# Turned heads scored on 32x32 tiles in 14 units, in an attention and MLP block on one core

## The chip, the cores and the metric

The kernel runs on one core of one Trainium2 chip. The metric is the device time of one execution in microseconds (us). Before the change it is 1140.88 us, the median of three runs (1139.4 to 1143.8). Engines are named as the profile names them: PE (TensorE matmuls), PEld (its weight loads), DVE (VectorE), ACT (ScalarE), POOL (GpSimd) and SP (SyncE, which issues most DMAs here).

## The reference

A token block of 2048 rows and 448 columns goes through an attention and an MLP in parallel, and both are added to the input:

```python
B, S, D, H = 1, 2048, 448, 16      # Dh = 28, F = 1792
xn = layernorm(x)
# attention: 16 query heads, one key head and one value head
q = (xn @ wq).reshape(B, S, H, Dh).transpose(0, 2, 1, 3)
k, v = xn @ wk, xn @ wv
p = softmax(einsum("bhqd,bkd->bhqk", q, k) * Dh ** -0.5)
a = einsum("bhqk,bkd->bhqd", p, v) merged over heads @ wo
# MLP on a second layernorm of xn
h = gelu(layernorm(xn) @ w1 + b1)
return x + a + h @ w2 + b2
```

All data are float32.

## The kernel before

**Stages.** The first stage (to about 66 us) normalises the input, projects queries, keys and values and writes the queries to DRAM (`qd`). The second stage (to 454 us) is the MLP. The third is attention. Matmuls with the large operands run as float32r, with each operand held as a rounded high part and a low part (`w1h` and `w1l`, `hh` and `hl`, the rows of `ks` and of the query tiles), so that three products stand for one. The order on every engine is the program's own (`manual_schedule`): each engine takes its instructions in the order in which the code issues them, and waits at one whose input or buffer isn't free.

**Units and steps.** Attention has 16 units: four chunks of 512 queries (`NCH`) times four groups of four heads (`NG`). A unit goes through the 16 key tiles of 128 in 8 steps of two key tiles, so there are 128 steps, n = 0 to 127. For a key tile and a head, a score matmul writes 128 keys by 512 queries into one PSUM bank (the line `pe.matmul(s, ...)`, L798), ACT takes the exp out of it into a tile `p` (L805), and `pv` (L708) multiplies `p` with the values. One step issues 8 float32 matmuls of `pv` in one burst, on four column tiles of 32; they belong to the step before. A string, `ORDER`, gives the order within a step letter by letter: s a score with its exp, m a maximum, t a turned score, P the burst, e a turned exp, n a piece of the unit's normalisation, o a piece of the output projection.

**Maxima.** The softmax's maximum of each query is found ahead by a second set of score matmuls with queries on the partitions (`max_stream`, L478) and a reduction of each on DVE (L479). They are issued in the MLP stage, `MLP_MAX` = 15 for each 46 steps of the MLP's own matmul stream, and the rest in attention, spread by `weight`. `load_max` transposes a unit's maxima (L461) and DMAs them, negated, into a row of the query tile that meets a row of ones in `ks`. So the score comes out with the maximum taken off.

**Turned heads.** In 7 of the 16 units (`TURNED`) the fourth head goes another way. Its scores are computed with the queries on the partitions (`turned_scores`, L730, four matmuls for each of four query tiles), DVE copies them out of PSUM and takes their maximum in the same instruction (L731), and ACT takes the exp in place (L750). Sixteen DMAs per query tile then regroup the rows (`regroup`, L746), so that DVE's 32x32 block transposes (`turn_blocks`, L757) make the tiles `p` that `pv` needs. Such a head needs neither maximum matmuls nor score matmuls.

**PSUM.** Of eight banks `mp` has three (named m: maxima, turned scores, output tiles, transposes), `sp` four (scores) and `op` one (the sum of `pv`).

**MLP.** `mlp1` makes a 128x512 piece of the hidden layer by 11 matmuls, GELU and rounding on ACT, and the low half `hl` on DVE (L524, put off to the next slot through `lows`). `mlp2` uses it two slots later. A slot is one such piece. There are 56.

**Ones.** Two rows of `ks` are set to one by GpSimd (`ones_rows`, L389) after the keys have been loaded.

Of the kernel before, what the change touches and what calls it, by code (L numbers as in the profile page):

```python
# [15 lines left out]
P = 128  # L16
# [10 lines left out]
MLP_MAX = 15  # L27
ORDER = "smsmstnsPemssmosmnsm"
TURNED = (3, 5, 7, 9, 11, 13, 15)
QB = 8  # L30
RAWS = 3
# [6 lines left out]
def block_kernel(ctx, tc, x, wq, wk, wv, wo, w1, b1, w2, b2, out):  # L38
# [82 lines left out]
    for t in qmt:  # L121
        pool.memset(f(t), 0.0)
    b1r = wqp.tile([NF, P], F32, name="b1r", bufs=1)
# [21 lines left out]
    def split_weights():  # L145
        for i in range(2):
            split_small(kvraw[:, :, i, :], lambda w, i=i: w[:, :, 32 * i + 1:32 * i + 1 + DH])
# [159 lines left out]
    def w2_split(s):  # L307
        raw = wl_q.pop(0)
        ab = slice(2 * s, 2 * s + 2)
        act.activation(w2h[:, ab, :], raw, AF.Copy)  # L310
        dve.tensor_sub(w2l[:, ab, :], raw, f(w2h[:, ab, :]))

    def q_slot(c, i):
# [7 lines left out]
        def evac():  # L321
            qe = wqp.tile([P, 2, CW], F32R, name="qe", bufs=CT)
            at = slice(64 if i == 0 else 0, P)
            act.activation(qe[at, 0, :], ps[at, :], AF.Copy)
            vt = None
            if i == 0:
                vt = wqp.tile([32, CW], F32, name="vt", bufs=1)
                kl = wqp.tile([64, CW], F32R, name="kl", bufs=1)
                act.activation(ks[32:64, cols], ps[32:64, :], AF.Copy)
                act.activation(vt, ps[0:32, :], AF.Copy)  # L330
            dve.tensor_sub(qe[at, 1, :], ps[at, :], f(qe[at, 0, :]))
            if i == 0:
                dve.tensor_sub(kl[32:64, :], ps[32:64, :], f(ks[32:64, cols]))
                for dst, src in ((0, kl[32:64, :]), (64, kl[32:64, :]), (96, ks[32:64, cols])):
                    nc.sync.dma_start(f(ks[dst:dst + 32, cols]), f(src))
# [51 lines left out]
    def ones_rows():  # L387
        for r in (32, 96):
            pool.memset(f(ks[r:r + 1, :]), 1.0)  # L389

    later(3, 2, ones_rows, True)
# [4 lines left out]
    def load_m(u, j, qm=None, t=None):  # L396
        c, g = units[u]
        at = slice(0, CW) if t is None else slice(t * P, (t + 1) * P)
        cols = slice(c * CW + at.start, c * CW + at.stop)
        if qm is None:  # L400
            qm = qmt[heads.index((u, j)) % 3]
        for blk, i in ((1, 0), (2, 0), (0, 1), (3, 1)):
            nc.sync.dma_start(f(qm[32 * blk + 1:32 * blk + 1 + DH, at]), qd[i][DH * (4 * g + j):DH * (4 * g + j + 1), cols])
# [36 lines left out]
    def load_q(u):  # L440
# [6 lines left out]
        for blk, i in ((1, 0), (2, 0), (0, 1), (3, 1)):  # L447
            nh = heads_of(u)
            src = qd[i][4 * DH * g:4 * DH * g + DH * nh, cols].rearrange("(j r) n -> r j n", r=DH)
            nc.sync.dma_start(f(qs[32 * blk + 1:32 * blk + 1 + DH, 0:nh, :]), src)  # L450
# [6 lines left out]
    def load_max(u):  # L457
# [4 lines left out]
        mn = keep.tile([4 * CT, 2, P], F32R, name="mn", bufs=2)[0:nh * CT]  # L462
        act.activation(mn[:, 0, :], pm, AF.Copy, scale=-1.0)
        dve.scalar_tensor_tensor(mn[:, 1, :], pm, -1.0, f(mn[:, 0, :]), op0=ALU.mult, op1=ALU.subtract)
        nc.sync.dma_start(f(qs[32:33, 0:nh, :]), f(mn[:, 0, :]))
        nc.sync.dma_start(f(qs[96:97, 0:nh, :]), f(mn[:, 1, :]))

    def max_stream():
        for h, (u, j) in enumerate(heads):
# [5 lines left out]
            for t in range(CT):  # L475
                for n in range(4):
# [3 lines left out]
                    if (j, t, n) == (heads_of(u) - 1, CT - 1, 3):  # L480
                        mrs[u] = keep.tile([P, 4 * CT], F32, name="mr", bufs=10)
# [31 lines left out]
    def mlp1(c, ft):  # L513
# [10 lines left out]
        lows.append(lambda: dve.tensor_sub(hl, hr, f(hh)))  # L524

    def mlp2(c, ft, between):
# [4 lines left out]
        for k in range(CT):  # L531
# [11 lines left out]
            if k == 2 and lows:  # L543
                lows.pop(0)()
            yield

    def slot(n):
# [13 lines left out]
        else:  # L561
            if nxt:
                nxt()
            lows.pop(0)()

    lows, norms, maxed = [], {}, 0
# [34 lines left out]
    q3 = att.tile([P, CW], F32R, name="q3", bufs=1)  # L601
    pool.memset(f(q3), 0.0)
# [32 lines left out]
    def norm_jobs(u, po):  # L635
# [12 lines left out]
        else:  # L648
            nc.sync.dma_start(rc, oc[0:P:32, :])
            yield  # L650
            yield
# [68 lines left out]
    turned, tside = {}, Stream()  # L720

    def turned_scores(u):
        turned[u] = hbs = []
        nxt = TURNED.index(u) + 1
        for t in range(CT):
            raw = att.tile([P, 4, NT, 32], F32, name="raw", bufs=RAWS)
            m3 = att.tile([P, 8], F32, name="m3")
            for n in range(4):
                sc = mtile([P, CW])
                pe.matmul(sc, q3[:, t * P:(t + 1) * P], ks[:, n * CW:(n + 1) * CW], start=True, stop=True)  # L730
                dve.tensor_scalar(raw[:, :, 4 * n:4 * n + 4, :].rearrange("p r b i -> p b r i"),  # L731
                                  sc.rearrange("p (b r i) -> p b r i", r=4, i=32), SCALE, -3e38,
                                  op0=ALU.mult, op1=ALU.max, accum_out=m3[:, n:n + 1])
                if n == 3:
                    dve.tensor_reduce(m3[:, 4:5], m3[:, 0:4], axis=AX.X, op=ALU.max, negate=True)  # L735
                    tside.add(turned_exps(hbs, t, raw, m3))
                    if nxt < len(TURNED):
                        load_m(TURNED[nxt], 3, q3, t)
                yield

    def turned_exps(hbs, t, raw, m3):
        def regroup(r):
            if t % 2 == 0 and r == 0:
                hbs.append(half_tile())
            for a in range(4):
                nc.sync.dma_start(hbs[-1][32 * r:32 * r + 32, 4 * (t % 2) + a, :],  # L746
                                  raw[32 * a:32 * a + 32, r].rearrange("p b i -> p (b i)"))

        for r in range(4):
            act.activation(raw[:, r], raw[:, r], AF.Exp, bias=m3[:, 4:5], scale=1.0)  # L750
            regroup(r)
            yield
# [10 lines left out]
    load_m(TURNED[0], 3, q3)  # L763
    tq = Stream()
    for u in TURNED:
        tq.add(turned_scores(u))

    def o_wait(c, gs, tiles):
        for _ in range(8):
# [7 lines left out]
    weight = [0 if n >= len(steps) - LEAD else 8 if u in TURNED  # L777
              else 18 if u + 2 < NU else 12 for n, (u, kt) in enumerate(steps)]
    for n, (u, kt) in enumerate(steps):
        if n == 12:  # L780
            prep_wo()
        if u + 1 < NU:
            if kt == 0:
                load_q(u + 1)
        qs = qss[u]
        j = 0
        for what in ORDER:
            if what == "s":
                kk = kt + j // 4
                if u in TURNED and j % 4 == 3:  # L790
                    if j == 3:
                        p = pair_of()
                        turn_blocks(p, u, kt)
                        ps[u, kt, 3], ps[u, kt + 1, 3] = p[:, 0], p[:, 1]
# [16 lines left out]
            elif what == "t":  # L811
                if n >= 3:
                    tq.step()
            elif what == "e":
                if kt == (6 if u + 2 < NU else 10) and u + 1 < NU:
                    load_max(u + 1)
                tside.step()
            elif what == "n":
                side.step()
            elif what == "o":  # L820
# [7 lines left out]
            elif n > 0 and 2 * n % BURST == 0:  # L828
                for _ in range(BURST):
                    pv(*pvq.pop(0))  # L830
# [29 lines left out]
```

## Time and profile before

| what | us |
|---|---|
| median of three runs | 1140.88 |
| the profiled execution, its time | 1142.51 |
| the profiled execution, its span | 1140.7 |
| first score matmul of attention | 454.54 |
| first value burst | 460.24 |

The trace is of one execution. A row of the groups gives line, engine, operation, what it writes and reads, shapes and count, then busy time in us and the mean duration in ns, then the idle time of that engine just before and what ended it. Durations overlap, since a matmul's or an activation's tail runs beside the next one's start. So what an instruction costs a busy engine is read from start to start. The granted TensorE clock is 0.998 over the span.

### The profile page before, as it was taken

How to read it: one execution, taken by the hardware profiler on the slowest of the kernel's cores; microseconds unless marked ns; L12 is line 12 of the kernel's file. 1: busy time of each engine (PE TensorE's matmuls, PEld its weight loads, DVE VectorE, ACT ScalarE, POOL GpSimd, SP SyncE). 2: the span in 40 equal slices, each digit the busy share in tenths (PEclk: the TensorE clock that was granted, in tenths of full speed). 3: DMA queues.
4: the chain of work that ended last, by engine and by line, in shares of the span. 5: the costliest groups of instructions: out<-in, count | busy, mean ns of one | idle time of the engine just before them, and what ended most of it. 6: DMA issues, size and time to landing. Idle time of an engine off the chain costs nothing.

```text
span 1140.7 us, 17019 instructions
## 1 busy us (share of the span) xinstructions
PE 1122.8 (98%) x5905; PEld 729.7 (64%) x5905; DVE 867.1 (76%) x1600; ACT 689.6 (60%) x1290; POOL 109.3 (10%) x113
## 2 busy tenths in 40 slices
PE   9989999999999999999999999999999999999998
PEld 8768888888888888555554555544455554564454
DVE  7779889888888888777777777777667677777434
ACT  6753322221222222788888877888777888878974
POOL 5340000000002000002101101101101101101100
PEclk9999999999999999999999999999999999999999
DMA  9751100000000020332343342342433443442300
GB/s 287 200 181 51 43 15 17 17 17 18 17 17 17 17 49 18 86 82 75 97 100 78 101 111 76 105 100 74 103 97 84 102 101 76 106 104 65 85 24 33
DMA packets 65426, 86.82 MB, mean 76 GB/s; under 512 B 20566, under 2 KB 31980, under 8 KB 65212
## 3 DMA queue, kind: packets, MB, share of 16 engines
q1 hardware_dynamic: 63932, 85.16, 28.1%
q8 instruction: 47, 0.77, 0.3%
q10 hardware_dynamic: 1408, 0.57, 0.2%
q14 instruction: 39, 0.32, 0.1%
HBM read 44.05 MB, written 11.12 MB: 48 GB/s over the span
## 4 chain that ended last, share of the span: by engine, by line
PE 88%; DVE 4%; DMA 3%; ACT 2%; issue 1%; SPq 1%; POOL 0%; DVEq 0%; ACTq 0%; POOLq 0%
PE po L708 19%; PE m L478 18%; PE s L798 17%; PE ph L158 10%; PE m L535 4%; PE m L537 4%; PE m L533 4%; PE m L730 3%; DMA xh<-qd 2%; PE qp L158 2%; PE m L622 1%; PE m L624 1%; PE m L623 1%; PE ph L161 1%; DMA rc<-oc 1%
## 5 line engine op out<-in xcount | busy, mean ns | idle before, releaser
L479 DVE TENSOR_REDUCE mx<-m 128x1 f32<-128x512 f32 x912 | 593.2, 685 | 160.5 <-PE m L478 146.2
L805 ACT ACTIVATE p<-s 128x512 f32<-128x512 f32 x879 | 447.4, 614 | 94.3 <-PE s L798 94.2
L478 PE MATMUL m<-ks,qm 128*128 128x512 f32 x912 | 371.0, 407 | 3.5 <-POOL ks L389 2.4
L798 PE MATMUL s<-xh,ks 128*128 128x512 f32 x879 | 318.2, 407 | 2.8 <-ACT p L805 2.5
L708 PE MATMUL po<-p,vs 128*32 128x512 f32 x2048 | 247.9, 601 | 0.0
L478 PEld LDWEIGHTS m<-ks,qm 128*128 128x128 f32 x912 | 171.3, 188 | 108.5 <-issue 26.0
L798 PEld LDWEIGHTS s<-xh,ks 128*128 128x128 f32 x879 | 163.3, 188 | 86.6 <-ACT p L805 35.0
L519 ACT ACTIVATE hr<-ph,b1t 128x512 f32<-128x512 f32 x56 | 38.6, 689 | 277.3 <-PE ph L163 191.5
L708 PEld LDWEIGHTS po<-p,vs 128*32 128x32 f32 x2048 | 53.9, 109 | 120.2 <-issue 114.1
L750 ACT ACTIVATE raw<-raw,m 128x512 f32<-128x512 f32 x112 | 82.7, 738 | 9.9 <-DVE m L735 9.0
L533 PE MATMUL m<-w2h,hh 128*128 128x448 f32 x224 | 82.4, 368 | 0.0
L535 PE MATMUL m<-w2l,hh 128*128 128x448 f32 x224 | 81.6, 364 | 0.0
L537 PE MATMUL m<-w2h,hl 128*128 128x448 f32 x224 | 81.5, 364 | 0.0
L731 DVE TENSOR_SCALAR_CACHE_REDUCE raw<-m 128x512 f32<-128x512 f32 x112 | 76.2, 680 | 0.0
L660 POOL TENSOR_TENSOR oc<-oc,tr 128x512 f32<-128x512 f32 x15 | 19.4, 1294 | 589.0 <-DMA tr<-ld 206.6
L757 DVE STREAM_TRANSPOSE p<-half 128x512 f32<-128x512 f32 x112 | 72.6, 687 | 1.6 <-PE po L708 1.6
L158 PE MATMUL ph<-xh,w1h 128*128 128x512 f32 x168 | 66.5, 396 | 0.0
L158 PE MATMUL ph<-xh,w1l 128*128 128x512 f32 x168 | 66.4, 395 | 0.0
L158 PE MATMUL ph<-xl,w1h 128*128 128x512 f32 x168 | 66.0, 393 | 0.0
L626 DVE TENSOR_TENSOR acc<-acc,m 128x448 f32<-128x448 f32 x22 | 13.6, 621 | 51.5 <-PE m L624 51.5
L730 PE MATMUL m<-ks,q 128*128 128x512 f32 x112 | 47.2, 422 | 3.4 <-DVE mx L479 3.4
L535 PEld LDWEIGHTS m<-w2l,hh 128*128 128x128 f32 x224 | 42.0, 188 | 6.3
(141 smaller groups left out, 964.4 us busy)
## 6 DMA issues: line engine op xcount, KB each, us to landing
half<-raw SPq DMA_DIRECT2D x448, 64.0 KB
qm<-qd SPq DMA_DIRECT2D x228, 56.0 KB
xh<-qd SPq DMA_DIRECT2D x36, 224.0 KB
qd<-qe SPq DMA_DIRECT2D x24, 256.0 KB
xh<-qd SPq DMA_DIRECT2D x28, 168.0 KB
tr<-ld SPq DMA_DIRECT2D x56, 64.0 KB
raw<-in_B_w_dram SPq DMA_DIRECT2D x7, 448.0 KB
out_dram<-acc SPq DMA_DIRECT2D x14, 224.0 KB
```

The lines of the kernel that those rows point to most:

```text
L158: pe.matmul(ps, w, v, start=(n == 0), stop=False)
L478: pe.matmul(pm, qm[:, t * P:(t + 1) * P], ks[:, n * CW:(n + 1) * CW], start=True, stop=True)
L479: dve.tensor_reduce(mx[:, CT * j + t, n:n + 1], pm, axis=AX.X, op=ALU.max)
L533: pe.matmul(m2[k], hh[:, ts], w2h[:, ft, :], start=(ft == 0), stop=False)
L535: pe.matmul(m2[k], hh[:, ts], w2l[:, ft, :], start=False, stop=False)
L537: pe.matmul(m2[k], hl[:, ts], w2h[:, ft, :], start=False, stop=(ft == NF - 1))
L708: pe.matmul(po[32 * j:32 * j + 32, :], vs[:, kt, :], ps.pop((u, kt, j)), start=(kt == 0), stop=(kt == NT - 1))
L730: pe.matmul(sc, q3[:, t * P:(t + 1) * P], ks[:, n * CW:(n + 1) * CW], start=True, stop=True)
L731: dve.tensor_scalar(raw[:, :, 4 * n:4 * n + 4, :].rearrange("p r b i -> p b r i"), sc.rearrange("p (b r i) -> p b r i", r=4, i=32), SCALE, ...
L750: act.activation(raw[:, r], raw[:, r], AF.Exp, bias=m3[:, 4:5], scale=1.0)
L798: pe.matmul(s, ks[:, kk * P:(kk + 1) * P], qs[:, j % 4, :], start=True, stop=True)
L805: act.activation(p, s, AF.Exp, scale=SCALE)
```

## The change

The set of turned units grows from 7 to 14 (units 2 to 15). Their scores are computed in float32 by 16 matmuls on 32x32 tiles for one query tile of 128: row group a of the array holds 32 queries of block a, column group r takes every fourth key block of 32, and the results land in four banks in the layout that the block transposes need. So the 16 regrouping DMAs go. Float32 keys come from `kf`, the sum of the high and low rows of `ks`, made once by GpSimd; queries come from `q3s`, summed from DMAs of both parts (`load_q3`, 8 DMAs a unit). A query's maximum is now spread over four partitions, so two small transposes on PE with a reduction and two copies on DVE join it (`turned_max`, letters c and d). The rounds (letter R) stand in odd steps from n = 7 to 117, the maxima in even steps from unit 2 on, and a turned exp (letter x) is issued twice a step. All scores, maxima, rounds and transposes take their banks in turn from one ring of seven. `MLP_MAX` goes to 20; the MLP's low halves `hl`, and the low halves `w2l` but the first, are computed by GpSimd. `ks` is set to one as a whole at the start, with 28 rows of keys copied instead of 32.

```diff
-MLP_MAX = 15
-ORDER = "smsmstnsPemssmosmnsm"
-TURNED = (3, 5, 7, 9, 11, 13, 15)
+MLP_MAX = 20
+ORDERS = ("scsmsmsxPdemsxmsmnsmson", "ssmssxRPesxmsnsson")
+TURNED = tuple(range(2, 16))
...
+    pool.memset(f(ks), 1.0)
...
-        dve.tensor_sub(w2l[:, ab, :], raw, f(w2h[:, ab, :]))
+        (pool if s else dve).tensor_sub(w2l[:, ab, :], raw, f(w2h[:, ab, :]))
...
-    def ones_rows():
-        for r in (32, 96):
-            pool.memset(f(ks[r:r + 1, :]), 1.0)
-
-    later(3, 2, ones_rows, True)
...
-        lows.append(lambda: dve.tensor_sub(hl, hr, f(hh)))
+        pool.tensor_sub(hl, hr, f(hh))
...
-        return att.tile([P, QB, CW], F32, name="half", bufs=3)
+        return att.tile([P, QB, CW], F32, name="half", bufs=4)
+
+    banked = 0
+
+    def mtile(shape):
+        nonlocal banked
+        banked += 1
+        return mp.tile(shape, F32, name="m") if banked % 7 in (1, 2, 3) else sp.tile(shape, F32, name="s")
...
+    for n in range(4):
+        cols = slice(n * CW, (n + 1) * CW)
+        pool.tensor_add(kf[:, cols], f(ks[:, cols]), kt_[:, n, :])
+    kq = kf.rearrange("p (b r i) -> p b r i", r=4, i=32)
...
+    def load_q3(u):
+        c, g = units[u]
+        for i, q in enumerate(q3p):
+            src = qd[i][DH * (4 * g + 3):DH * (4 * g + 4), c * CW:(c + 1) * CW].rearrange("r (t g j) -> g r t j", g=4, j=32)
+            for b in range(4):
+                nc.sync.dma_start(q[32 * b:32 * b + DH, :, :], src[b])
+        q3s[u] = att.tile([P, CT, 32], F32, name="q3s", bufs=2)
+        pool.tensor_add(q3s[u], q3p[0], q3p[1])
+
+    def turned_round(u, t):
+        if t % 2 == 0:
+            turned.setdefault(u, []).append(half_tile())
+        half = turned[u][-1]
+        banks = [mtile([P, CW]) for _ in range(4)]
+        for r in range(4):
+            for a in range(4):
+                pe.matmul(banks[a][32 * r:32 * r + 32, :], q3s[u][32 * a:32 * a + DH, t, :],
+                          kq[32 * a:32 * a + DH, :, r, :], start=True, stop=True)
+        m3 = att.tile([P, 4], F32, name="m3")
+        for a in range(4):
+            dve.tensor_scalar(half[:, 4 * (t % 2) + a, :], banks[a], SCALE, -3e38,
+                              op0=ALU.mult, op1=ALU.max, accum_out=m3[:, a:a + 1])
+        maxes.append(turned_max(half, t, m3))
+
+    def turned_max(half, t, m3):
+        pt = mtile([4, P])
+        pe.transpose(pt, m3, ident)
+        mq = att.tile([4, 4, 32], F32, name="mq", bufs=1)
+        dve.tensor_reduce(mq[:, 0, :], pt.rearrange("a (r j) -> a j r", r=4), axis=AX.X, op=ALU.max, negate=True)
+        dve.tensor_copy(mq[:, 1:4, :], mq[:, 0:1, :].to_broadcast([4, 3, 32]))
+        yield
+        pb = mtile([P, 4])
+        pe.transpose(pb, mq.rearrange("a r j -> a (r j)"), ident[0:4, 0:4])
+        mb = att.tile([P, 4], F32, name="mb")
+        dve.tensor_copy(mb, pb)
+        for a in range(4):
+            exps.append((half[:, 4 * (t % 2) + a, :], mb[:, a:a + 1]))
+        yield
+
+    def turned_exp():
+        if exps:
+            raw, m = exps.pop(0)
+            act.activation(raw, raw, AF.Exp, bias=m, scale=1.0)
...
-    weight = [0 if n >= len(steps) - LEAD else 8 if u in TURNED
-              else 18 if u + 2 < NU else 12 for n, (u, kt) in enumerate(steps)]
+    weight = [0 if n >= len(steps) - LEAD else 2 if u == 0 or u == 1 and n % 2 == 0 else 1 if u == 1 or n % 2 == 0
+              else 0 for n, (u, kt) in enumerate(steps)]
+    rounds = {8 * (u - 2) + 7 + 2 * t: (u, t) for u in TURNED for t in range(CT)}
...
-        for what in ORDER:
+        if u in TURNED:
+            while exps and kt == 0:
+                turned_exp()
+            p = pair_of()
+            turn_blocks(p, u, kt)
+            ps[u, kt, 3], ps[u, kt + 1, 3] = p[:, 0], p[:, 1]
+        for what in ORDERS[n % 2 if n > 6 else 0]:
...
-                s = mtile([P, CW]) if (n == 0 and j < 3) or (maxed == total and j % 2) else sp.tile([P, CW], F32, name="s")
+                s = mtile([P, CW])
...
+            elif what == "R":
+                if n in rounds:
+                    turned_round(*rounds[n])
+            elif what in "cd":
+                if maxes:
+                    next(maxes[0])
+                    if what == "d":
+                        maxes.pop(0)
+            elif what == "x":
+                turned_exp()
+                if kt == 14 and len(exps) == 1:
+                    turned_exp()
...
+            elif what == "P":
+                for _ in range(BURST if n else 0):
+                    pv(*pvq.pop(0))
```

Counted over the kernel: 912 maximum and 912 score matmuls become 800 and 800, 112 turned score matmuls become 56 rounds of 16, 448 regrouping DMAs go, and the turned exps, the copies out of PSUM and the block transposes on DVE go from 112 to 224 each.

More of the change, by code (lines that the diff above doesn't have):

```diff
@@ L542, in mlp2 @@
                 between()
-            if k == 2 and lows:
-                lows.pop(0)()
             yield
@@ L718, in pv @@
                 oside.add(o_wait(c, range(NG), range(CT if c < NCH - 2 else 2)))
[L720 to L744, printed above, removed]
-            for a in range(4):
[L746 to L752, printed above, removed]
+    turned, q3s, maxes, exps = {}, {}, [], []
```

70 lines of the change are left out of this document (29 added, 41 removed).

## The prediction

> **What bounds the kernel now.** I read the page first (shares of the span, then the chain that ended last), then the busy times by stage, then the groups by line, and last the timeline of two steps of the attention stage.
>
> ```profile
> span 1140.7 us, 17019 instructions
> PE 1122.8 (98%) x5905; PEld 729.7 (64%) x5905; DVE 867.1 (76%) x1600; ACT 689.6 (60%) x1290; POOL 109.3 (10%) x113
> ...
> PE 88%; DVE 4%; DMA 3%; ACT 2%; issue 1%; SPq 1%; POOL 0%; DVEq 0%; ACTq 0%; POOLq 0%
> ```
>
> TensorE is busy all the time and is 88% of the chain. A share over the whole span hides the stages, so here they are (columns: stretch, length, then busy us and count on PE, PEld, DVE, ACT, POOL; granted clock; DMA).
>
> ```profile
> 66.00:454.30 388.30, 385.13 (x1761) 323.80 (x1760) 337.17 (x534) 97.28 (x148) 26.83 (x21) 1.00 0.10 29
> 460.20:504.50 44.30, 44.29 (x246) 23.38 (x245) 32.46 (x61) 34.91 (x71) 0.00 (x0) 1.00 0.32 77
> 504.50:550.20 45.70, 44.94 (x246) 23.33 (x245) 33.41 (x65) 39.56 (x80) 7.61 (x7) 1.00 0.38 95
> 550.20:1077.60 527.40, 521.94 (x2929) 269.86 (x2928) 386.04 (x755) 425.18 (x828) 41.65 (x39) 1.00 0.37 93
> 1077.60:1128.30 50.70, 50.70 (x306) 27.95 (x305) 16.59 (x28) 37.96 (x76) 2.59 (x2) 1.00 0.06 18
> 1128.30:1140.70 12.40, 7.68 (x47) 4.60 (x46) 6.06 (x14) 2.11 (x5) 0.00 (x0) 0.98 0.21 75
> ```
>
> The first stretch is the MLP; the others are attention, cut at the value bursts that open steps 0, 8, 16, 116 and 127 (a step is two key tiles of one unit; a unit has 8). In the MLP DVE stands at 337 of 388 us and ACT is nearly free. In attention ACT is at 80%, DVE at 73%. A step of a turned unit, on PE:
>
> ```profile
> 694.51 0.63 PE L798 MATMUL s<-xh,ks 128*128 128x512 f32 x2
> ...
> 695.90 0.40 PE L730 MATMUL m<-ks,q 128*128 128x512 f32 x1
> 696.22 1.92 PE L708 MATMUL po<-p,vs 128*32 128x512 f32 x16
> 698.08 1.20 PE L798 MATMUL s<-xh,ks 128*128 128x512 f32 x4
> 699.11 0.40 PE L478 MATMUL m<-ks,qm 128*128 128x512 f32 x1
> 699.35 0.47 PE L798 MATMUL s<-xh,ks 128*128 128x512 f32 x1
> ...
> 700.47 1.06 PE L708 MATMUL po<-p,vs 128*32 128x512 f32 x8
> ```
>
> From burst to burst are 4.25 us. A burst lasts 1.86 (696.22 to 698.08), it starts 0.32 after the last matmul's start, and a 512-column matmul costs about 0.235: nine of them with a burst are 4.1, so PE sets the pace. ACT at the same place:
>
> ```profile
> 691.73 0.71 ACT L750 ACTIVATE raw<-raw,m 128x512 f32<-128x512 f32 x1
> 692.35 1.05 ACT L805 ACTIVATE p<-s 128x512 f32<-128x512 f32 x2
> 694.94 2.07 ACT L805 ACTIVATE p<-s 128x512 f32<-128x512 f32 x4 [1.55 <-PE s L798]
> 696.87 0.74 ACT L750 ACTIVATE raw<-raw,m 128x512 f32<-128x512 f32 x1
> ```
>
> A score matmul started at 694.51 and its exp at 694.94: 0.43 of latency. Exps follow each other by 0.48 (696.87 less 694.94, over 4), a turned exp takes 0.62 of the queue (692.35 less 691.73), and before the row of four ACT idled 1.55 us.
>
> **The change part by part.** *Front.* The 2048-column memset of ks moves ahead of GpSimd's first split:
>
> ```profile
> 1.73 1.46 POOL L122 MEMSET qm<- 128x512 f32 x3
> 6.25 0.29 POOL L141 TENSOR_SCALAR wah<-kvraw 128x112 fp32r<-128x112 f32 x1 [3.06 <-DMA kvraw<-in_A_wv_dram]
> ...
> 66.24 3.65 POOL L389 MEMSET ks<- 1x2048 f32 x2 [3.24 <-DVE qe L331]
> ...
> 69.95 0.50 PE L478 MATMUL m<-ks,qm 128*128 128x512 f32 x1 [2.44 <-POOL ks L389]
> ```
>
> One such memset is 3.65/2 = 1.8 us and fits the 3.06 idle (nothing; at most 1.8 if the weights landed earlier). The two late ones go, and with them PE's wait of 2.4 (0 if another wait stands right behind): -2.4.
>
> *MLP.* Of 1288 steps of the MLP stream, 20 instead of 15 in 46 carry a maximum matmul: 140 more, at 0.235, +33. First burst: 460.2 + 33 - 2.4 = 491. Cover on DVE:
>
> ```profile
> L479 DVE TENSOR_REDUCE mx<-m 128x1 f32<-128x512 f32 x912 | 593.2, 685 | 160.5 <-PE m L478 146.2
> L524 DVE TENSOR_TENSOR hl<-hr,hh 128x512 fp32r<-128x512 f32 x56 | 40.4, 722 | 0.0
> L311 DVE TENSOR_TENSOR w2l<-raw,w2h 128x896 fp32r<-128x896 f32 x7 | 7.6, 1080 | 0.0
> L667 POOL TENSOR_TENSOR otl<-oc,oth 128x512 fp32r<-128x512 f32 x15 | 19.3, 1288 | 4.4 <-ACT oth L664 3.2
> ```
>
> A reduction costs DVE 593.2/912 = 0.65, so 140 add 91, and 47 leave for GpSimd: 381 of 419 us, still below PE. GpSimd takes 1.29 for a low half (row L667), 56 of them are 72 us in 419, and the matmul that reads one comes two slots (14 us) later: nothing. Without that cover DVE would pace the stage at about +10.
>
> *Attention, units 0 and 1.* Unit 0: 8 scores, 6 maxima and a burst, 14 x 0.235 + 1.95 = 5.24 a step, 43 with its ends (44.3 now). Unit 1 gets four rounds as well; a pair of its steps has 16 exps and 4 turned exps, 16 x 0.48 + 4 x 0.62 = 10.2 of ACT. At the densest ACT in the trace,
>
> ```profile
> 1050.00:1100.00 50.00, 49.71 (x284) 25.26 (x283) 20.91 (x39) 43.23 (x85) 3.99 (x4) 1.00 0.28 72
> ```
>
> 43.23 of 50 or 86%, that is 11.8, and the queue below makes it 12.5: 49 for the unit (45.7 now).
>
> *The round.* 16 float32 matmuls take the place of four 0.235 ones for seven turned heads, and of 32 (16 maxima, 16 scores) for seven new ones. The nearest row is the burst, also float32 and also on tiles:
>
> ```profile
> 642.26 0.13 PEld L708 LDWEIGHTS po<-p,vs 128*32 128x32 f32 x4 [0.30 <-issue]
> 642.69 0.13 PEld L708 LDWEIGHTS po<-p,vs 128*32 128x32 f32 x4 [0.30 <-issue]
> 643.66 0.28 PE L461 MATMUL m<-ident,mr 128*12 128x128 f32 x1
> 643.69 0.48 PE L478 MATMUL m<-ks,qm 128*128 128x512 f32 x1
> ```
>
> Each of 8 float32 matmuls is recorded twice (x16), and four column tiles go together in waves 0.43 apart. If all 16 tiles run together, a round is two waves: a burst less two waves, 1.86 - 0.86 = 1.0 until the next burst starts. If the four row groups go one after another it is 8 waves, 1.86 + 4 x 0.43 = 3.6. I take 1.0, because the four column tiles share their waves without loss. The switch into tiles is the 0.32 against 0.235, about 0.1 a round. The Trainium skill, TensorE: Matmul & The Clock Gate, section Measured speedup vs the span model, gives 10.6 times for 16 such tiles; against 16 x 0.86 in series that is an estimate of 1.3 a round, and 1198 in all by it; no run here shows it. The two small transposes a round adds cost PE 0.03 to 0.06 (643.66 to 643.69).
>
> *A pair of steps from unit 2 on* (all units turned): 12 scores, 3 maxima, 2 bursts, 1 round, 2 transposes. PE: 15 x 0.235 + 2 x 1.95 + 1.1 + 0.1 = 8.6. ACT: 12 x 0.48 + 4 x 0.62 = 8.24. DVE, by these rows,
>
> ```profile
> L731 DVE TENSOR_SCALAR_CACHE_REDUCE raw<-m 128x512 f32<-128x512 f32 x112 | 76.2, 680 | 0.0
> L731 DVE DVE_READ_ACCUMULATOR raw<-m 128x1 f32 x112 | 9.2, 82 | 0.0
> L757 DVE STREAM_TRANSPOSE p<-half 128x512 f32<-128x512 f32 x112 | 72.6, 687 | 1.6 <-PE po L708 1.6
> L735 DVE TENSOR_REDUCE m<-m 128x1 f32<-128x4 f32 x28 | 4.4, 158 | 1.0
> L805 ACT ACTIVATE p<-s 128x512 f32<-128x512 f32 x879 | 447.4, 614 | 94.3 <-PE s L798 94.2
> ```
>
> 3 x 0.65 + 4 x 0.76 + 4 x 0.65 (72.6/112) + about 0.6 for a reduction and two copies a round (an estimate from row L735's 0.16) = 8.2. Three engines stand within 0.4 us of each other, so the order decides. A pair takes 21 banks of the ring of seven, and a bank's next user waits for its reader. Counting seven back along the two orders, the round's fourth bank is that of the even step's last score: the round waits for that exp, which stands behind one turned exp in ACT's queue. The even step's second maximum (just ahead of its burst) waits for the exp of the odd step's second score behind the burst. That closes a loop, from the round's fourth matmul:
>
> - round 1.0, burst 1.86, latency 0.43, exp 0.48, turned exp 0.62, exp done 0.61 (row L805), PE wakes 0.06: 5.06
> - the maximum, switch and burst 0.32 + 1.86, transpose and a maximum 0.27, latency 0.43, exp 0.48, turned exp 0.62, exp 0.48, exp done 0.61, wake 0.06: 5.13
>
> The wake is read where a matmul waited for its bank:
>
> ```profile
> 1005.58 0.19 PEld L478 LDWEIGHTS m<-ks,qm 128*128 128x128 f32 x1 [0.20 <-DVE mx L479]
> 1005.64 0.44 PE L478 MATMUL m<-ks,qm 128*128 128x512 f32 x1
> ```
>
> Together 10.2 a pair, 1.6 over PE's sum. ACT then works 8.24 of 10.2, 81%, which the trace has reached; 8.6 would ask 96%, which no stretch shows. What ends last in this stage turns from PE to exps that start late after each burst.
>
> *Sum.* First burst 491, unit 0 43, unit 1 49, fifty pairs 510; 10 output tiles (12 matmuls of 448 columns, 0.235 x 448/512 = 0.2 each; of their 2.4 about 1.7 not in PE's waits) 17, and the copy that 13 units add on ACT, 0.6 like an exp, 8; the last 11 steps and the end, which hold the same work, 50.7 + 12.4. That makes 1181. The regroup transfers' removal frees SP and DMA, at a 0.37 share, which bounded nothing: 0. The profiled execution took 1142.5 for its span of 1140.7 and the median is 1140.9, so span and median agree: 1181.
>
> **Rivals.** *PE stays the bound; faster.* If exps run in the shadow of the bursts after all, a pair is 8.6 to 9: 491 + 42 + 44 + 440 + 30 + 63 = 1110. It decides from a pair below 9.4, where the sum is 1141. For it: PE paces a turned step exactly today, and all three sums are at most 8.6. Against: there ACT has 6 exps and one turned exp in 4.25 us, 82%, here two; and scores and maxima have banks of their own today.
>
> *The round is slow.* Row groups in pairs, 0.86 more: times 56 rounds: +48, 1229; in series, 2.6 more: +145, 1326. For: nothing in this trace runs on row tiles. Against: a burst's waves lose nothing over four column tiles.
>
> *It comes out even:* the 33 us given to the MLP come back in attention, a pair near 9.4: 1141.
>
> **How the numbers follow.** The ring's loop 0.57, PE-bound 0.19, slow round 0.2, even 0.04. The likeliest gives 1181; its own range, pairs of 9.7 to 10.5, is 1156 to 1196. To hold 8 in 10 the range takes in the PE-bound case nearly whole and the round in pairs: 1108 to 1235. Within 0.5% (1135 to 1147) a measurement of this kernel can't tell from no change. Faster 0.19, same 0.04, slower 0.77.
>
> **What would show it.** First burst at 489 to 493 and no PE wait on ks (MLP part). Bursts in units 2 to 13 with pairs of 10.2, PE busy below 90%, and PE's idle time before the round's matmul and before a maximum put down to ACT's exp (the loop); with DVE there instead, the evacuation paces. A round's 32 records within 0.6 us of starts (all tiles together), or in steps of 0.43 (row groups in turn). Wrong if PE stays at 97% in attention, or if the MLP stage grows by more than 38 us.

## The result and the profile after

The changed kernel takes 1214.1 us, the median of four executions (1208.57 to 1219.73), against 1141.97 for the kernel before beside it: ratio 1.0634, interval 1.0564 to 1.0703, so 6% slower. The granted clock was 0.95 in two of these four, the profiled one among them, and 1.0 in the other two. A second measurement of the same kernel, at the full clock throughout like all experiments below, gave 1208.66 (1208.47 to 1209.21), ratio 1.0604 [1.0586, 1.0622]. The experiments are compared with it, and its profile (the second execution, span 1206.7) is the one that is read.

The page of the first execution: span, shares, and the shares of the chain that ended last.

```profile
span 1217.2 us, 19933 instructions
PE 1187.6 (98%) x7473; PEld 716.2 (59%) x7473; DVE 926.9 (76%) x1902; ACT 703.3 (58%) x1290; POOL 202.1 (17%) x193
...
PE 6%; DVE 0%; ACT 0%; issue 0%; DVEq 0%
```

The shares look like those of before: PE at 98%. The chain could be followed over only 6% of the span here, so it doesn't answer the 88% of before. What replaces both is the table by stage of the second execution, columns as before, cut at the same bursts (two rows: the MLP, and steps 16 to 116):

```profile
66.00:485.00 419.00, 418.01 (x1897) 349.46 (x1897) 390.73 (x613) 97.35 (x148) 106.66 (x81) 1.00 0.10 32
...
588.50:1144.80 556.30, 536.92 (x4193) 231.01 (x4197) 386.48 (x947) 436.10 (x824) 46.97 (x51) 1.00 0.12 32
```

The MLP of the first execution, for the last section:

```profile
66.00:485.00 419.00, 417.99 (x1897) 349.51 (x1896) 390.50 (x612) 97.17 (x147) 106.77 (x81) 0.95 0.11 31
```

Three stretches grew. The first burst comes at 490.9 instead of 460.2: +30.7. Steps 16 to 116 take 556.3 instead of 527.4: +28.9. Units 0 and 1 take 97.6 instead of 90.0. In the long stage PE reads as busy for 536.92 of 556.3 us, yet its matmuls did not fill that time. The groups of weight loads of the second execution show it: the row of a load carries the idle time ahead of it and what ended that.

```profile
L471 PEld LDWEIGHTS m<-ks,qm 128*128 128x128 f32 x658 | 123.5, 188 | 46.7 <-ACT p L823 19.6 <-DVE mx L472 9.0 <-issue 1.7
L471 PEld LDWEIGHTS s<-ks,qm 128*128 128x128 f32 x142 | 26.6, 187 | 25.7 <-ACT p L823 21.9 <-issue 1.7
L744 PEld LDWEIGHTS s<-kf,q3s 28*32 28x32 f32 x1024 | 20.8, 103 | 40.6 <-ACT p L823 33.2 <-issue 6.5 <-DVE rc L658 0.4
L744 PEld LDWEIGHTS m<-kf,q3s 28*32 28x32 f32 x768 | 17.1, 103 | 22.9 <-ACT p L823 11.4 <-issue 10.8 <-DVE rc L658 0.4
```

Exps on ACT (L823) held back the rounds (L744) for 33.2 + 11.4 = 44.6 us and the maxima (L471) for 19.6 + 21.9 = 41.5 us. These are the two waits of the predicted loop. Here is one pair of steps in the timeline of the second execution, from burst to burst.

```profile
772.73 0.16 PEld L714 LDWEIGHTS po<-p,vs 128*32 128x32 f32 x8 [0.24 <-issue]
774.58 0.13 PEld L760 LDWEIGHTS s<-ident,mq 4*128 4x128 f32 x1 [0.84 <-DVE mx L472]
774.73 0.19 PEld L471 LDWEIGHTS m<-ks,qm 128*128 128x128 f32 x1
775.07 0.63 PE L816 MATMUL m<-xh,ks 128*128 128x512 f32 x2
775.50 0.60 ACT L823 ACTIVATE p<-m 128x512 f32<-128x512 f32 x1 [0.69 <-PE m L816]
775.99 0.71 ACT L770 ACTIVATE half<-half,mb 128x512 f32<-128x512 f32 x1
776.56 1.73 PE L744 MATMUL m<-kf,q3s 28*32 28x512 f32 x6
776.61 0.59 ACT L823 ACTIVATE p<-m 128x512 f32<-128x512 f32 x1
777.09 2.06 ACT L823 ACTIVATE p<-s 128x512 f32<-128x512 f32 x4
777.25 0.13 PEld L744 LDWEIGHTS m<-kf,q3s 28*32 28x32 f32 x2 [0.55 <-ACT p L823]
777.73 0.10 PEld L744 LDWEIGHTS s<-kf,q3s 28*32 28x32 f32 x1 [0.35 <-ACT p L823]
778.80 1.92 PE L714 MATMUL po<-p,vs 128*32 128x512 f32 x16
780.68 0.71 PE L816 MATMUL s<-xh,ks 128*128 128x512 f32 x2
781.20 0.60 ACT L823 ACTIVATE p<-s 128x512 f32<-128x512 f32 x1
781.69 0.72 ACT L770 ACTIVATE half<-half,mb 128x512 f32<-128x512 f32 x1
782.31 0.59 ACT L823 ACTIVATE p<-s 128x512 f32<-128x512 f32 x1
782.95 0.19 PEld L471 LDWEIGHTS s<-ks,qm 128*128 128x128 f32 x1 [0.70 <-ACT p L823]
783.38 1.93 PE L714 MATMUL po<-p,vs 128*32 128x512 f32 x16
```

Follow the bank. The round's fourth matmul (777.73) waits for an exp that could start only at 777.09, behind a turned exp (775.99) and two others, all of which start after the burst. The maximum at 782.95 waits in the same way for the exp of 782.31, behind the turned exp of 781.69. One pair is 783.38 - 772.73 = 10.65 us.

### The profile page after: what moved, and what is told of

The parts are those of the page before. It is cut to its first block, busy times and chain, and to the rows that moved or that the text cites. A ratio compares the mean times of both kernels' runs of the same rounds, so it can differ in the third digit from the quotient of the medians.

```text
span 1217.2 us, 19933 instructions
## 1 busy us (share of the span) xinstructions
PE 1187.6 (98%) x7473; PEld 716.2 (59%) x7473; DVE 926.9 (76%) x1902; ACT 703.3 (58%) x1290; POOL 202.1 (17%) x193
## 5 line engine op out<-in xcount | busy, mean ns | idle before, releaser
L472 DVE TENSOR_REDUCE mx<-m 128x1 f32<-128x512 f32 x658 | 431.0, 687 | 38.8 <-PE m L471 33.5
L823 ACT ACTIVATE p<-s 128x512 f32<-128x512 f32 x464 | 255.1, 607 | 79.7 <-PE s L816 79.1
L471 PE MATMUL m<-ks,qm 128*128 128x512 f32 x658 | 267.8, 407 | 10.6 <-ACT p L823 9.6
L823 ACT ACTIVATE p<-m 128x512 f32<-128x512 f32 x336 | 188.0, 607 | 61.0 <-PE m L816 60.3
L770 ACT ACTIVATE half<-half,mb 128x512 f32<-128x512 f32 x224 | 162.9, 734 | 0.0
L816 PE MATMUL s<-xh,ks 128*128 128x512 f32 x464 | 158.6, 414 | 0.2
L471 PEld LDWEIGHTS m<-ks,qm 128*128 128x128 f32 x658 | 123.5, 188 | 46.8 <-ACT p L823 19.6
L816 PE MATMUL m<-xh,ks 128*128 128x512 f32 x336 | 113.7, 406 | 0.7 <-ACT p L823 0.7
L744 PE MATMUL s<-kf,q3s 28*32 28x512 f32 x1024 | 100.8, 617 | 0.0
L472 DVE TENSOR_REDUCE mx<-s 128x1 f32<-128x512 f32 x142 | 92.8, 676 | 9.4 <-PE s L471 9.0
L744 PE MATMUL m<-kf,q3s 28*32 28x512 f32 x768 | 93.3, 617 | 0.0
```

The costliest lines, as they stand in the source:

```text
L471: pe.matmul(pm, qm[:, t * P:(t + 1) * P], ks[:, n * CW:(n + 1) * CW], start=True, stop=True)
L472: dve.tensor_reduce(mx[:, CT * j + t, n:n + 1], pm, axis=AX.X, op=ALU.max)
L744: pe.matmul(banks[a][32 * r:32 * r + 32, :], q3s[u][32 * a:32 * a + DH, t, :], kq[32 * a:32 * a + DH, :, r, :], start=True, stop=True)
L770: act.activation(raw, raw, AF.Exp, bias=m, scale=1.0)
L816: pe.matmul(s, ks[:, kk * P:(kk + 1) * P], qs[:, j % 4, :], start=True, stop=True)
L823: act.activation(p, s, AF.Exp, scale=SCALE)
```

## The experiments

Stages are cut at the bursts of steps 0, 16 and 116, as before (us; "end" is from step 116 to the span's end). The times are medians, except in the first row; the stages are read from the one profiled execution of each run.

| run | time | ratio to before | first burst | units 0, 1 | steps 16-116 | end |
|---|---|---|---|---|---|---|
| before, profiled | 1142.51 | 1 | 460.2 | 90.0 | 527.4 | 63.1 |
| b1_again | 1208.66 | 1.0604 [1.0586, 1.0622] | 490.9 | 97.6 | 556.3 | 61.9 |
| a1_exps_last | 1156.46 | 1.0146 [1.0130, 1.0162] | 491.2 | 96.0 | 505.3 | 62.0 |
| a2_no_turned_exp | 1146.58 | 1.0058 [1.0042, 1.0073] | 491.0 | 92.1 | 499.6 | 62.0 |
| a3_max15 | 1183.58 | 1.0383 [1.0366, 1.0399] | 454.5 | 97.5 | 567.7 | 62.0 |
| a4_max15_exps_last | 1146.10 | 1.0053 [1.0034, 1.0072] | 455.2 | 96.1 | 531.7 | 61.9 |
| b2_odd_exp_last | 1182.66 | 1.0374 [1.0358, 1.0389] | 491.1 | 96.1 | 531.8 | 61.9 |
| b3_scores_first | 1167.87 | 1.0246 [1.0230, 1.0261] | 492.1 | 101.1 | 511.3 | 62.2 |
| b4_scores_first_max16 | 1194.68 | 1.0480 [1.0464, 1.0495] | 461.0 | 100.8 | 568.9 | 62.2 |
| c1_lows_on_vector | 1225.77 | 1.0755 [1.0733, 1.0776] | 507.7 | 97.6 | 556.2 | 61.9 |
| c2_seven_units | 1177.66 | 1.0333 [1.0313, 1.0353] | 490.4 | 85.9 | 536.0 | 63.3 |
| c3_before_lows_on_gpsimd | 1136.72 | 0.9975 [0.9964, 0.9986] | 456.2 | 89.4 | 524.7 | 63.1 |
| c4_seven_units_max15 | 1168.10 | 1.0251 [1.0231, 1.0272] | 453.7 | 89.5 | 559.6 | 63.3 |

The medians of before beside them were 1139.64 (a), 1140.84 (b) and 1139.31 (c).

### Where the turned exp stands in ACT's queue

**a1_exps_last.** The second turned exp of each step is issued behind the step's last score exp instead of after the first score behind the burst. No work is removed.

```diff
-ORDERS = ("scsmsmsxPdemsxmsmnsmson", "ssmssxRPesxmsnsson")
+ORDERS = ("scsmsmsxPdemsmsmnsxmson", "ssmssxRPesmsnsxson")
```

> The second turned exp of each step moves behind the step's last score exp in ACT's queue; nothing else changes. Loop theory (the ring makes the round wait for the even step's last exp, and the second maximum for the odd step's second one, each behind one turned exp): 0.62 us leave the loop twice, a pair of steps goes from 10.8 to about 9.6, 56 rounds, so about 65 us faster than the changed kernel (1150 us). Rival, ACT's total work sets the pace: no change beyond 5 us, since ACT does the same work. Rival, the round on row tiles is slow: no change.

Measured: 1156.46, 52 us less than 1208.66, all of it in attention's stages. (The 65 expected had been worked out from the first execution's pair of 10.8 and for 56 of them.) The groups of weight loads of this run:

```profile
L471 PEld LDWEIGHTS s<-ks,qm 128*128 128x128 f32 x142 | 26.6, 187 | 6.8 <-issue 1.7 <-ACT p L823 0.5
L744 PEld LDWEIGHTS s<-kf,q3s 28*32 28x32 f32 x1024 | 20.1, 103 | 22.4 <-ACT p L823 16.1 <-issue 5.9 <-DVE mx L472 0.2
L744 PEld LDWEIGHTS m<-kf,q3s 28*32 28x32 f32 x768 | 16.9, 103 | 17.9 <-issue 7.7 <-ACT p L823 7.0 <-DVE mx L472 1.7
```

The maxima hardly wait for an exp any more (0.5 us on the row that had 21.9, and at most 0.8 on the row that had 19.6), and the rounds half as long (23.1 instead of 44.6). In its timeline the exps after the burst of 765.27 run without a turned exp between them:

```profile
768.05 0.60 ACT L823 ACTIVATE p<-m 128x512 f32<-128x512 f32 x1 [0.16 <-PE m L816]
768.54 1.08 ACT L823 ACTIVATE p<-s 128x512 f32<-128x512 f32 x2
769.49 0.73 ACT L770 ACTIVATE half<-half,mb 128x512 f32<-128x512 f32 x1
769.67 0.10 PEld L744 LDWEIGHTS s<-kf,q3s 28*32 28x32 f32 x1 [0.36 <-ACT p L823]
```

The round's fourth matmul comes 769.67 - 765.27 = 4.40 after the burst, against 777.73 - 772.73 = 5.00: a turned exp's 0.6 less. A pair is 9.48 instead of 10.65.

**a2_no_turned_exp.** The turned exps are left out altogether, so the weights of the turned heads stay raw scores; everything else is as in the changed kernel.

```diff
-            act.activation(raw, raw, AF.Exp, bias=m, scale=1.0)
+            pass
```

> The exp of the turned heads is left out altogether (224 activations of about 0.62 us, 139 us of ACT). Loop theory: only the two that stand in the loop count, so about the same as with the exps moved behind, 65 to 80 us faster than the changed kernel (1135 to 1150). Rival, ACT's total work sets the pace: ACT falls from 8.24 to 5.76 a pair, PE's sum of 8.7 takes over, 115 us faster (1100). Rival, the round is slow: no change.

Measured: 1146.58. Taking the whole of this work from ACT is worth 62 us, and moving half of it by a few places is worth 52. So it was the place in the queue and not ACT's load: in steps 16 to 116 of a1 ACT does the same work as in the changed kernel, and the stage is 51 us shorter. The ring still binds in a2. Its pairs take 9.54 (one runs from the burst of 768.78 to that of 778.31), no less than the 9.48 of a1. The round of that pair, and the burst behind it:

```profile
772.61 0.62 PE L744 MATMUL m<-kf,q3s 28*32 28x512 f32 x2
773.24 0.10 PEld L744 LDWEIGHTS s<-kf,q3s 28*32 28x32 f32 x1 [0.35 <-ACT p L823]
774.30 1.92 PE L714 MATMUL po<-p,vs 128*32 128x512 f32 x16
```

The round's fourth bank still waits for the even step's last exp, which now stands behind two other exps alone. From the round's first matmul to the burst are 774.30 - 772.61 = 1.69. A round that nothing holds up takes 1.15 (shown further below), so PE's own sum is about 9.54 - 0.54 = 9.0 a pair (an estimate).

**b2_odd_exp_last.** Only the odd step's turned exp is moved.

```diff
-ORDERS = ("scsmsmsxPdemsxmsmnsmson", "ssmssxRPesxmsnsson")
+ORDERS = ("scsmsmsxPdemsxmsmnsmson", "ssmssxRPesmsnsxson")
```

> Only the odd step's second turned exp moves behind its last score exp. Loop theory: one of the two waits in the loop is shortened, the second maximum's, by 0.62 us a pair: half of the gain of both, about 26 us faster than the changed kernel. Rival, only the round's wait counts and the maximum's is hidden behind it: no change, and all of the gain belongs to the even step.

Measured: 1182.66, which is 26.0 less than 1208.66, half of a1's 52.2. The rows of the weight loads say which half: the maxima's wait for exps falls from 21.9 to 1.0 us on their second row, and the rounds' stays, 33.0 + 12.5 = 45.5 against 44.6. Each of the loop's two waits carries its own half.

**b1_again** is the changed kernel itself, run with these.

> The changed kernel, unchanged, once more. Its four executions so far stood at 1209 with a granted clock of 0.999 and at 1219 with 0.949, two each. If the low clock belongs to the chip that it ran on, all runs here stand at 1205 to 1210 with 0.999; if it belongs to the kernel, half of them stand at 1219 again. At full clock the loop should be 10.6 to 10.7 us a pair against the 10.8 of the first profile.

Measured: 1208.66 at a clock of 1.0 in all four executions. The lower clock did not come back, but four executions are too few to rule out that it belongs to the kernel.

### What the maxima cost on either side

**a3_max15** and **a4_max15_exps_last.** The MLP carries 15 maxima per 46 steps of its stream as before, in the changed order and in that of a1. (46 steps are two slots; "a slot" in the expectations stands for them.)

```diff
-MLP_MAX = 20
+MLP_MAX = 15
```

> The MLP carries 15 instead of 20 maximum matmuls per 46 steps, as before the change; about 138 maxima go back to attention, some 2.8 more a pair. Loop theory: PE waits 1.6 us or more in every pair and takes them there almost for nothing: the MLP gets 33 us shorter, attention at most 12 longer, so 20 to 33 us faster than the changed kernel (1181 to 1194). Rival, PE sets the pace of attention: what the MLP wins attention loses, within 5 us of the changed kernel.

> Both edits. Loop theory: the loop is down to 9.6 a pair and PE's sum is up to about 9.3 with the maxima, so the two gains add up but for some 15 us: 1130 to 1145, level with the kernel before the change. Rival, PE or ACT sets the pace: 1205 to 1220.

Measured: 1183.58 and 1146.10. The traces have 568 maximum matmuls ahead of the first burst with 20 and 430 with 15, so 138 move, not quite the 140 of the prediction. The MLP is shorter by 490.9 - 454.5 = 36.4 for them, 0.26 each. In attention they cost 567.7 - 556.3 = 11.4, or 0.08 each, in the changed order, which has idle PE time to put them in, and 531.7 - 505.3 = 26.4, or 0.19 each, in the order of a1. Both are less than the MLP pays. The 20 maxima were therefore a loss of some 25 us in the kernel as it stands and of 10 once its order is mended. a4 is just over its expected range (1130 to 1145): up to unit 5 its pairs take 10.85, with eight maxima in each, and only then 9.57.

**b3_scores_first** and **b4_scores_first_max16.** A third order: the even step issues its remaining scores right behind the burst, and the maxima after them, so that the exps start as early as they can. b4 does so with 16 maxima per 46 steps.

```diff
-ORDERS = ("scsmsmsxPdemsxmsmnsmson", "ssmssxRPesxmsnsson")
+ORDERS = ("scsmsxsPssssdmmxmenmmon", "ssssxRPssssxemnmon")
```

> Behind each burst the three scores come first, then the transposes and the maxima, and the turned exp last; one maximum stays ahead of the even step's burst. The round's banks then wait for maxima on DVE that are done early and no longer for the last exp. Loop theory: PE's own sum of about 8.9 us a pair, with a rest of 0.3 of waits, against 9.5 with the exps moved alone: 1135 to 1145. Rival, ACT's total work (8.3 us a pair) can't go over 86% of the time: it stays at 9.5 a pair, 1156.

> The same order with 16 maxima per 46 steps in the MLP. Loop theory: the MLP is 26 us shorter; attention gets 2.2 more maxima a pair, which cost PE 0.5 each pair where nothing waits and less in the rest of the round's wait: level with scores first alone or up to 10 us faster, 1125 to 1145. Rival, DVE now ends last (9.1 us a pair with 5.2 maxima): 10 to 20 us slower than scores first alone.

Measured: 1167.87 and 1194.68, both above what either theory expected, though b4's rival had named the right engine. The exps do come early, but the loop closes over DVE. The timeline of b3 from the burst at 774.59 to the next:

```profile
774.59 1.92 PE L714 MATMUL po<-p,vs 128*32 128x512 f32 x16
775.58 1.28 DVE L775 STREAM_TRANSPOSE p<-half 128x512 f32<-128x512 f32 x2
776.79 0.24 DVE L756 TENSOR_REDUCE mq<-m 4x32 f32<-4x128 f32 x1
777.23 0.67 DVE L472 TENSOR_REDUCE mx<-s 128x1 f32<-128x512 f32 x1
778.11 1.29 DVE L472 TENSOR_REDUCE mx<-s 128x1 f32<-128x512 f32 x2
779.45 0.10 PEld L744 LDWEIGHTS s<-kf,q3s 28*32 28x32 f32 x1 [0.38 <-DVE mx L472]
780.52 1.92 PE L714 MATMUL po<-p,vs 128*32 128x512 f32 x16
```

The round's banks are now those of the maxima, and it waits for DVE, whose queue holds block transposes, the turned maximum and three reductions: 779.45 - 774.59 = 4.86, against 4.40 in a1. The waits of the rounds' loads in b3 and then in b4:

```profile
L744 PEld LDWEIGHTS s<-kf,q3s 28*32 28x32 f32 x1024 | 18.5, 103 | 17.6 <-DVE mx L472 11.5 <-issue 3.8 <-ACT p L823 1.9
L744 PEld LDWEIGHTS m<-kf,q3s 28*32 28x32 f32 x768 | 16.8, 103 | 18.3 <-DVE mx L472 9.0 <-ACT p L823 5.5 <-issue 3.8
```

```profile
L744 PEld LDWEIGHTS s<-kf,q3s 28*32 28x32 f32 x968 | 20.8, 103 | 31.4 <-DVE mx L472 23.3 <-issue 5.0 <-ACT p L823 1.3
L744 PEld LDWEIGHTS m<-kf,q3s 28*32 28x32 f32 x824 | 17.9, 103 | 25.3 <-DVE mx L472 18.2 <-issue 6.7
```

ACT is down to 7.4 us in b3 and 1.3 in b4's row, and DVE stands at 20.5 and 41.5. b4 puts 111 more maxima into steps 16 to 116 (269 against 158), which cost (568.9 - 511.3)/111 = 0.52 each, nearly a whole reduction on DVE. A maximum that stands between the burst and the round lies on the loop; the same maximum cost 0.08 to 0.19 in a3 and a4. b3 also lost 3.5 us in units 0 and 1 against the changed kernel, which was not followed up.

### GpSimd's part

**c1_lows_on_vector** is the changed kernel with `hl` back on VectorE; **c3_before_lows_on_gpsimd** is the kernel before with that part of the change alone.

```diff
-        pool.tensor_sub(hl, hr, f(hh))
+        lows.append(lambda: dve.tensor_sub(hl, hr, f(hh)))
...
+            if k == 2 and lows:
+                lows.pop(0)()
```

> The changed kernel with the MLP's 56 low halves back on VectorE, 20 maxima a slot kept. By the prediction VectorE then paces the MLP stage: the first burst about 10 us later (near 501 instead of 490.9), the rest as it was, so 1217 to 1221 against 1208.7 at the full clock. Rival: the stage is bound by TensorE's 20 maxima alone and GpSimd's part is worth nothing: first burst within 2 us of 491, time 1207 to 1211.

> The kernel before with one part of the change alone: the 56 low halves on GpSimd, 15 maxima a slot, seven turned units as before. From the first bursts at 15 maxima (460.2 before, 454.5 and 455.2 in the changed kernels) about 5 us faster: ratio 0.995 to 0.997. Rival: that difference came from other parts (the ones rows, the ring) and TensorE is the bound of the stage anyway (385.8 of 389 us busy): no difference, ratio 0.999 to 1.001.

Measured: c1 takes 1225.77, 17.1 more than the changed kernel (some 10 had been expected), and its first burst comes 16.8 later. Its MLP stage, columns as before:

```profile
66.00:501.00 435.00, 423.10 (x1895) 347.96 (x1894) 414.24 (x668) 97.80 (x148) 36.04 (x25) 1.00 0.10 31
```

DVE stands at 414.24 of 435 us, PE idles 12, and the loads of the maxima wait 28.7 us for DVE's reductions in this stage, against 9.0 in the changed kernel. At 20 maxima per 46 steps the move to GpSimd is worth these 17 us. In the kernel before, at 15, it is worth a little by itself: c3 has its first burst 4.0 us earlier than the profiled execution of before, and takes 0.9975 [0.9964, 0.9986] of the time of before over ten executions, a little less of a gain than the 0.995 to 0.997 expected. It is the only version here that beats the kernel before, by 2.6 us.

### The number of turned units

**c2_seven_units** has the order of a1 with the seven odd units turned; **c4_seven_units_max15** has 15 maxima per 46 steps as well, and two more places for a maximum.

```diff
-ORDERS = ("scsmsmsxPdemsxmsmnsmson", "ssmssxRPesxmsnsson")
-TURNED = tuple(range(2, 16))
+ORDERS = ("scsmsmsxPdemsmsmnsxmson", "ssmssxRPesmsnsxson")
+TURNED = (3, 5, 7, 9, 11, 13, 15)
```

(In c4 the odd step is "ssmssxRPemsmsnsmxson".)

> The changed kernel with the turned exps last (as in a1_exps_last, 1156.5) and the turned heads back in the seven odd units, 20 maxima a slot. TensorE's count: a pair that isn't turned has 4 scores and 4 maxima more (8 x 0.235 = 1.9) and no round, which costs 1.1 + 0.1 of switch + about 0.4 for its two transposes and their switches = 1.6, so 0.3 a pair, 28 pairs: +8 us, about 1165 (1157 to 1172). Rival one: a turned head is worth what it is worth in the kernel before (units of 36.6 us against 43.6 to 45.5, 7 to 8 us each): +50, about 1206. Rival two: the ring of banks and the ACT queue still end last in turned pairs and are gone in the others: faster than 1150.

> Exps last, 15 maxima a slot and the seven odd units turned: against the kernel before there remain the round of 16 float32 matmuls in place of four of 0.235, GpSimd and the ring. If a round costs TensorE 1.6 against 0.94, 28 rounds cost +19, and the low halves give back 5: 1150 to 1160. If the fourteen units are what costs and the round itself is free, it ends at or below the kernel before: 1130 to 1141. If the maxima of nine whole units (432 left to attention) crowd VectorE: 1165 or more.

Measured: 1177.66 and 1168.10. Against the runs with fourteen units (1156.46 and 1146.10) that is 21.2 and 22.0 more, so about 3 us for each of seven units. (c4 also has its two more places for a maximum.) In the kernel before, a turned unit took 36.6 to 36.8 us (units 3, 7 and 11) and one that isn't 43.7 to 45.5 (units 2, 4, 6 and 10): 7 to 8 apart. So a turned head is still a gain in the new way, two fifths of what it was. The larger number of units is not what made the kernel slow. c2 lies above its range of 1157 to 1172. c4 differs from the kernel before in the turned round, GpSimd's part, the ring and the order, and takes 28.8 us more. Its time is the one expected for a crowded VectorE (1165 or more), but its trace doesn't show that cause. Steps 16 to 116, columns as before:

```profile
543.20:1102.80 559.60, 554.13 (x3725) 280.54 (x3724) 396.80 (x822) 426.39 (x832) 44.27 (x45) 1.00 0.14 39
```

DVE is busy for 396.80 of 559.60 us, and no group of weight loads waits more than 3.4 us in all for its reductions. The round's own time is a small part: 28 rounds of 1.15 (below) for 112 matmuls of 0.235 are 32.2 - 26.3 = 6 us more (an estimate without the transposes). How the rest divides between the units that carry the rounds, the ring and the order stays open.

## Why the prediction held, and where its sizes were off

**The range.** The mechanism was right and its price too low. The loop's own forecast was 1181, with a range of 1156 to 1196, and both measurements, 1214.1 and 1208.66, lie above it. They lie inside 1108 to 1235 because that range had been widened upwards for a round that goes in pairs of row groups, which did not happen.

**MLP.** First burst at 491 was predicted, and 490.9 came. The sum is closer than its terms: the maxima cost 36.4 (33 predicted), the ones rows and what goes with them give 456.2 - 454.5 = 1.7 (2.4), and the low halves give 4.0, which the prediction took as nothing, since it looked only at cover and not at the gain. The maxima cost 3.4 more than predicted and the ones rows gave 0.7 less, and the 4.0 that had been left out cancels them, so the hit is partly luck. DVE's sum was 381 and reads 390.73. Without the cover +10 was foreseen; c1 shows +16.8.

**The loop.** The mechanism is shown by a1, a2 and b2: both waits stand at the places named, the round's fourth bank and the even step's second maximum, and each is behind one turned exp. Its size was 10.2 and is 10.65 (times from the pair shown above):

| from | to | predicted | measured |
|---|---|---|---|
| round's fourth matmul | burst | 1.0 | 1.07 |
| burst | first score | 1.86 | 1.88 |
| score | exp | 0.43 | 0.52 |
| exp, turned exp | next exp | 1.10 | 1.11 |
| exp's start | maximum's load | 0.67 | 0.64 |
| maximum | burst | 0.32 | 0.43 |
| burst | transpose | 1.86 | 1.85 |
| transpose | first score | 0.27 | 0.49 |
| score | exp | 0.43 | 0.43 |
| three queue places | fourth exp | 1.58 | 1.59 |
| exp's start | round's fourth matmul | 0.67 | 0.64 |

Two terms carry most of the 0.46. Behind the burst the small transpose takes 0.15 (774.58 to 774.73), and the maximum after it 0.34 instead of 0.235 (774.73 to 775.07). And a maximum that had to wait takes 0.43 up to the burst (782.95 to 783.38); the 0.32 had been read where PE ran without a stop. (The first 0.52 belongs to this pair: a copy of the next unit's maxima, 780.97 to 781.24 on ACT, stands ahead of the exp.) Over fifty pairs the 0.46 is 23 us.

**What the prediction missed.** In the last step of each unit the order issues two turned exps in a row, and the loop takes both. In the second execution of the changed kernel:

```profile
802.97 1.32 ACT L770 ACTIVATE half<-half,mb 128x512 f32<-128x512 f32 x2
804.20 0.58 ACT L823 ACTIVATE p<-s 128x512 f32<-128x512 f32 x1
...
804.83 0.19 PEld L471 LDWEIGHTS s<-ks,qm 128*128 128x128 f32 x1 [1.31 <-ACT p L823]
```

PE's load waits 1.31 instead of 0.70, and that step takes 5.17 where the others take 4.57. Over some twelve units this is 7 us more. Units 0 and 1 were put at 92 and took 97.6. The output tiles and the copies were put at 25; what is left of the stage for them is 556.3 - 50 x 10.65 - 7 = 17. In all 23 + 7 + 5.6 - 8 = 28, and 1181 + 28 is the 1209 of the full clock.

**The round.** All 16 tiles run together, as was taken. In five rounds of the second execution nothing holds a bank, and the 32 records of such a round start within 0.63 us. One of them, and the first loads of the burst behind it:

```profile
718.80 1.22 PE L744 MATMUL s<-kf,q3s 28*32 28x512 f32 x32
719.95 0.16 PEld L714 LDWEIGHTS po<-p,vs 128*32 128x32 f32 x8 [0.84 <-issue]
```

From its first matmul to the burst are 1.15, and 1.07 from the fourth bank on where that one is waited for (777.73 to 778.80), against 1.0 taken. So the rival of a slow round falls. The Trainium skill's 10.6 times for 16 tiles (TensorE: Matmul & The Clock Gate, section Measured speedup vs the span model) had given an estimate of 1.3 a round; 1.15 was measured, so here the float32 round did better than that figure.

**The sign that failed.** "PE busy below 90%" was named as a sign and "PE stays at 97% in attention" as what would refute the loop. PE stays at 536.92 of 556.3, 96.5%, and the loop is there, so by this sign the prediction would have been given up although its mechanism held. In the pair shown above two of the round's matmuls start at 776.56, the third waits for its bank until 777.25 and the fourth until 777.73. The records of the first three (776.56, x6, two for each) reach over 1.73 us without a break, so the wait reads as PE time. The idle time on the weight loads and its releaser were the sign to name. The Trainium skill warns of this share for another reason (Perfetto Trace Analysis, section Identifying the Most-Contended Engine): matmul busy time is not a good measure of how close a kernel is to the peak, because pipelined matmuls look smaller in the trace. Here the share errs the other way. The page points to the share of weight loads instead, among others; it fell here from 269.86 of 527.4 us to 231.01 of 556.3, but the change also put small loads of 103 ns in the place of some of 188 ns, so it doesn't size the wait by itself.

**The other rivals.** "PE stays the bound, 1110" falls for the kernel as written. Its step that failed is the pair of 8.6: even with no turned exp at all (a2) a pair takes 9.54, of which PE's own sum is about 9.0 (estimated above), and the ring's wait is still in it. "Even, from a pair of 9.4" is nearly what a1 makes of it: a pair of 9.48, and a ratio of 1.0146.

**The balance.** From before to after at the full clock, by stage: MLP +30.7, units 0 and 1 +7.6, steps 16 to 116 +28.9, end -1.2, together 66.0, the difference of the spans 1206.7 and 1140.7. The third term is a gain of 22.1 (527.4 to 505.3) under a loss of 51.0 to the late exps (505.3 to 556.3). The gain is that of the maxima moved to the MLP: with them back, a4 takes 531.7, which is 4.3 more than before, though it has 99 maxima (295 for 394) and 104 scores (600 for 704) fewer there. So the turned units, with all that came with them, bring nothing in this stage against the kernel before. Without the late exps the kernel still doesn't pay (a1, 1.0146), because the MLP's 30.7 is more than the 22.1.

## What to carry to other kernels

Where several consumers share one ring of banks, count the ring back from every user to its last reader, and look at what stands ahead of that reader in its own engine's queue: a side job of 0.6 us at the wrong place cost 26 us here, and two places further on it cost the pair nothing (9.48 against 9.54 without it). Work moved into another stage to relieve a bound must be priced on both sides, for the same maximum cost 0.26 in the MLP, 0.08 to 0.19 in attention where PE had gaps, and 0.52 where it stood between a burst and a round. And a busy share near 100% doesn't say that an engine sets the pace, when its instructions can start and then wait for one another.

## What was not expected of the hardware

At a granted clock of 0.95 the value bursts slowed and the MLP did not. At the full clock a burst lasts 774.58 - 772.73 = 1.85; in the first profiled execution of the same kernel it lasts 657.67 - 655.75 = 1.92, by these rows of its timeline:

```profile
655.75 0.16 PEld L714 LDWEIGHTS po<-p,vs 128*32 128x32 f32 x8 [0.87 <-issue]
...
657.67 0.30 PEld L816 LDWEIGHTS s<-xh,ks 128*128 128x128 f32 x2 [0.88 <-issue]
```

Over 128 bursts the 0.07 is 9.0 of the 10.5 us between the two spans. Yet the first burst came at 490.7 and 490.9, and the 419 us of the MLP hold the same work in both (rows above). Why the clock was lower in two executions, and why the bursts followed it and the MLP did not, is not known from these runs.
